# Two stores of one attention and mixture kernel, divided by rows between two DMA queues

## The chip, the cores and the metric

The kernel runs on one core of a Trainium2 chip. A core has a matrix engine (TensorE, PE in the profile), a vector engine (VectorE, DVE), a scalar engine (ScalarE, ACT), a general engine (GpSimd, POOL) and one that does little but issue transfers (SyncE, SP). Sixteen DMA engines move data between the chip's memory and the core's on-chip memory, which has 128 rows, called partitions. Transfers are issued by GpSimd, SyncE or ScalarE, each with a queue of its own on the DMA engines. The metric is the device time of one execution in microseconds (us), less is better.

## The reference

Inputs are `q`, `k` and `v` of 4 x 6400 x 256 float32 numbers and small weights. The first half is attention across channels: with columns of `q` and `k` normed over the 6400 positions, each batch has a 256 x 256 matrix, its softmax, and a product with `v`. The second half sends each of the 25600 rows of that result to two of eight small experts.

```python
qn = q / (np.linalg.norm(q, axis=1, keepdims=True) + 1e-06)
kn = k / (np.linalg.norm(k, axis=1, keepdims=True) + 1e-06)
s = kn.transpose(0, 2, 1) @ qn / tau
...
x = v @ softmax(s)                        # then, by rows of x:
logits = x @ w_gate                       # the two largest of 8, softmax over them: w
out = x + sum over the two of w * ((x @ A[e]) @ B[e])
```

(The last three lines are a summary.) In bytes: three inputs of 26.2 MB are read and an output of 26.2 MB is written.

## The kernel before, in words

A batch's 6400 positions are laid out as 128 partitions of 50 rows, so that partition p holds positions 50p to 50p + 49. Work goes by "chunks", one row of every partition at a time.

For `q` and `k` of a batch there are three loads each (`QK`: 17, 17 and 16 chunks), some cut in two (`PARTS`). GpSimd issues them (`do_load`, L578) and they convert float32 to bfloat16 on the way. TensorE sums `k`-by-`q` products and diagonal norms in two accumulators (`do_G`, L593, L597, L602). Some norms are taken instead by ScalarE squares and VectorE sums (`do_sq` L615, `do_add` L621). At the end of a batch a short chain gives the softmax: `accs` (L651), `rsqrt`, `s` (L710), `exp` (ScalarE, L715), transposition (L729), and products with the weights (`waA`, L755, L757).

For `v` a batch has five loads of 10 chunks, also by GpSimd. A tile of `v` is transposed on TensorE (`do_T`, L788), copied (`do_Te`), multiplied by gate and expert weights (`ZL`, `log`, `Z`), gated on VectorE, and multiplied by the attention matrix (`do_Y`, L915 and L920). `do_Ye` copies the result into a `y` tile of 128 x 10 x 256 float32, by ScalarE (L769) or VectorE (L771). There are seven such tiles.

A `y` tile is stored as one transfer of 128 rows of 10240 bytes (`do_store`, L928), or, for the last two tiles of the last batch, in three parts. SyncE issues all stores, one behind the other. Tile (b, i) is the i-th of batch b.

The order of all this is not written by hand. `make_plan` lists every step with its dependencies, an estimated cost and a due time, `Plan.run` plays it through as a simulation and yields one list of steps, and the program emits them in that order; the order on each engine is then fixed. Some stores are held back on purpose: `HOLD` names a load for a store, and a tiny transfer by SyncE (`do_hold`, L645) waits for that load, so that this store and those behind it wait too. Tile (0, 2) is the first that is stored, at 76.65 us. Tile (0, 0) is held for the load of `k` (3, 1), and issued at 167.45 us.

Hardware queues tell completion by counts: a transfer adds sixteen in all to its semaphore, and the program uses eight such semaphores in turn for the transfers of SyncE and ScalarE. Whoever next writes a `y` tile waits until its store has completed.

Of the kernel before, what the change touches and what calls it, by code (L numbers as in the profile page):

```python
# [32 lines left out]
class Clock:  # L33


    WINDOW, FIRST, LOW, HIGH = 3.413, 0.31, 0.5, 0.8

# [3 lines left out]
    def at(self, t):  # L41
        w = max(0, int((t - self.FIRST) / self.WINDOW) + 1)
        while len(self.cold) <= w:
            share = self.busy[-1] / self.WINDOW
            self.cold.append(share < (self.HIGH if self.cold[-1] else self.LOW))
            self.busy.append(0.0)
        return w

    def took(self, t, us):

        end, w = t, self.at(t)
        while us > 1e-9:
            pace = 2.0 if self.cold[w] else 1.0
            step = min(us * pace, max(self.FIRST + w * self.WINDOW - end, 1e-6))
            self.busy[w] += step
# [5 lines left out]
    def idle(self, t):  # L61

        w = self.at(t)
        return t - self.FIRST - (w - 1) * self.WINDOW - self.busy[w] > self.SPARE

# [165 lines left out]
def make_plan(B, order, ahead):  # L231
# [150 lines left out]
    for b in range(B):  # L382
        for i in range(NP):
            x = pos["v", b, max(g for g, (i0, _) in enumerate(V) if i0 <= i)]
            parts = UNITS if b == B - 1 and i >= NP - FINE else ((0, PC),)
            for c, n in parts:
# [25 lines left out]

PARTS = {(0, 0): ((0, 2), (2, 15)), (0, 2): ((34, 8), (42, 8)), (3, 2): ((34, 8), (42, 8))}
FINE = 2
FIRST = 4
OFF = {(0, 0, 'k'), (0, 0, 'q'), (0, 1, 'q'), (0, 2, 'k'), (0, 2, 'q'), (0, 4, 'q'), (0, 5, 'q'),
        (0, 6, 'k'), (0, 6, 'q'), (0, 7, 'k'), (0, 8, 'q'), (1, 0, 'k'), (1, 0, 'q'), (1, 1, 'q'),
# [41 lines left out]
def kernel(  # L459
# [11 lines left out]
    nc = tc.nc  # L471

    B, N, C = q.shape
    P = 128
# [15 lines left out]
    out_v = out.rearrange("(b p c) d -> b p c d", b=B, p=P)  # L490
# [44 lines left out]
    held = {}  # L535
# [25 lines left out]
    def do_load(s, what, b, i, c, n):  # L561
        if what == "v":
            t, src, c0 = sb(s, "v", (b, i), [P, PC * max(n for _, n in V), C], BF16), v_v, c
        else:
            t = sb(s, "qk", (what, b, i), [P, max(n for _, n in QK), C], BF16)
            src, c0 = {"q": q_v, "k": k_v}[what], QK[i][0]
            if (b, c) == (0, 0):
                n = FIRST
                if "first" not in W:
# [6 lines left out]
        if (what, b, i) in (("q", 0, 0), ("k", 0, 0)):  # L576
            c, n = FIRST, c + n - FIRST
        nc.gpsimd.dma_start(t[:, c - c0:c - c0 + n, :], src[b, :, c:c + n, :])  # L578
# [346 lines left out]

    def do_store(s, b, i, c, n):
        lo = i * PC + c
        nc.sync.dma_start(out_v[b, :, lo:lo + n, :], held["y", (b, i), ""][:, c:c + n, :])  # L928


    do = dict(load=do_load, wts=do_wts, sq=do_sq, add=do_add, red=do_red, n2p=do_n2p, hold=do_hold, warm=do_warm, cast=do_cast, G=do_G, accs=do_accs, n2=do_n2, rsqrt=do_rsqrt, rq_ps=do_rq_ps, s=do_s,
              exp=do_exp, recip=do_recip, aT_ps=do_aT_ps, aT=do_aT, waA_ps=do_waA_ps, waA=do_waA,
              a=do_a, ZL=do_ZL, ZLe=do_ZLe, T=do_T, Te=do_Te, log=do_log, loge=do_loge, Z=do_Z, Ze=do_Ze, gzT=do_gzT,
              gzTe=do_gzTe, Y=do_Y, Ye=do_Ye, store=do_store)
    for name in ("m1", "eq1", "lm", "m2", "mask", "msum", "t", "th", "g2"):
        do[name] = gate_step(name)
# [50 lines left out]
```

## Time and profile before

| what | value |
|---|---|
| time, median of 3 runs | 254.43 us (254.37 to 254.54) |
| span of the profiled run | 252.7 us |
| TensorE busy | 217.8 us, 86% of the span |
| VectorE busy | 192.7 us, 76% |
| ScalarE busy | 151.1 us, 60% |
| GpSimd busy | 27.1 us, 11% |
| stores of 1280 KB by SyncE | 18, median 16.7 us from issue to landing |
| loads of `v` by GpSimd | 20 of 640 KB (as written), median 20.5 us to landing |
| ScalarE's own transfers | 3, all in the first 2 us |

The profile is of one execution. Busy times count an engine's instructions, and not what it spends on issuing transfers or waiting. The profile has the transfers by packet as well: their queue, their size, and when each began and ended. A queue is named q0 for GpSimd's loads, q1 for SyncE's transfers and q10 for ScalarE's; q8 and q14 fetch instructions for the engines themselves.

### The profile page before, as it was taken

What the parts mean: (1) busy time and instruction counts of PE and PEld (TensorE: products, weight loads), DVE (VectorE), ACT (ScalarE), POOL (GpSimd) and SP (SyncE); (2) the same over time, 40 slices, a digit from 0 to 9 for tenths busy, and PEclk for the clock granted to TensorE, in tenths of its full rate; (3) what the DMA queues carried; (4) which work ended last, traced back from release to release, by engine and by line L of the source; (5) the groups of instructions that cost most, each with busy time, mean ns of one, the idle gap of its engine ahead of it and who ended that gap; (6) DMA issues with size and microseconds to landing.
All of it is one profiled execution on the core that took longest, in us unless ns stands there. A gap on an engine that the chain in (4) does not pass through costs nothing.

```text
span 252.7 us, 5852 instructions
## 1 busy us (share of the span) xinstructions
PE 217.8 (86%) x2357; PEld 193.0 (76%) x2357; DVE 192.7 (76%) x528; ACT 151.1 (60%) x269; POOL 27.1 (11%) x54
## 2 busy tenths in 40 slices
PE   0274995988999998689999999889999979999990
PEld 0162882876999996579899899779999769999980
DVE  0055589869899987588899899489898898889850
ACT  5454427546786543975667768362674846657671
POOL 7003010040002002000500100500000000000000
PEclk9998899999999999999999999999999999999997
DMA  8999999999999999999999999999999999999996
GB/s 251 217 217 209 211 223 208 217 218 215 215 217 241 303 305 298 224 213 221 210 215 220 215 217 217 211 212 313 317 251 353 322 341 317 337 392 415 404 408 249
DMA packets 11243, 66.70 MB, mean 264 GB/s; under 512 B 1360, under 2 KB 1744, under 8 KB 6608
## 3 DMA queue, kind: packets, MB, share of 16 engines
q0 software_dynamic: 6912, 38.80, 74.4%
q1 hardware_dynamic: 3968, 26.87, 26.1%
q10 hardware_dynamic: 336, 0.66, 0.8%
q8 instruction: 18, 0.29, 0.4%
q14 instruction: 9, 0.07, 0.1%
HBM read 78.91 MB, written 26.21 MB: 416 GB/s over the span
## 4 chain that ended last, share of the span: by engine, by line
PE 53%; DMA 32%; issue 5%; DVE 4%; ACT 2%; POOL 1%; POOLq 0%; DVEq 0%
DMA v<-in_v_dram 18%; PE Y_ps L915 13%; PE acc L593 10%; DMA qk<-in_q_dram 10%; PE Y_ps L920 6%; PE T_ps L788 5%; PE ZL_ps L812 5%; DMA qk<-in_k_dram 5%; PE gzT_ps L902 4%; PE acc L597 3%; PE acc L602 2%; PE Z_ps L879 1%; ACT a_exp L715 1%; DVE a_bf L763 1%; PE log_ps L826 1%
## 5 line engine op out<-in xcount | busy, mean ns | idle before, releaser
L593 PE MATMUL acc<-qk 128*128 128x256 bf16 x400 | 69.6, 282 | 17.0 <-DMA qk<-in_k_dram 9.4
L915 PE MATMUL Y_ps<-a_bf,vT 128*128 128x256 bf16 x400 | 60.0, 273 | 0.2 <-DVE acc_sb L710 0.2
L621 DVE TENSOR_TENSOR ssq<-ssq,sq 128x1280 f32<-128x1280 f32 (+1 forms) x27 | 43.4, 1606 | 19.6 <-ACT sq L615 19.6
L769 ACT COPY y<-Y_ps 128x512 f32<-128x512 f32 x79 | 46.2, 586 | 16.6 <-PE Y_ps L920 13.5
L593 PEld LDWEIGHTS <-qk 128*128 128x128 bf16 x400 | 34.2, 101 | 20.7 <-DMA qk<-in_k_dram 11.5
L615 ACT ACTIVATE sq<-qk 128x1280 f32<-128x1280 bf16 (+1 forms) x27 | 36.9, 1368 | 17.7 <-DVE ssq L621 16.6
L915 PEld LDWEIGHTS <-vT 128*128 128x128 bf16 x400 | 38.9, 98 | 4.7 <-issue 0.3
L920 PE MATMUL Y_ps<-ball,gzT 128*128 128x256 bf16 x200 | 38.2, 273 | 0.0
L597 PE MATMUL acc<-qk 128*128 128x128 bf16 x242 | 34.5, 224 | 0.0
L788 PE MATMUL T_ps<-ident,v 128*128 128x128 f32 x200 | 27.6, 274 | 0.6 <-DVE waA_sb L757 0.4
L769 ACT COPY vT<-T_ps 128x512 f32<-128x512 f32 (+1 forms) x44 | 21.2, 510 | 10.9 <-PE T_ps L788 10.5
L597 PEld LDWEIGHTS <-qk 128*128 128x128 bf16 x242 | 24.4, 101 | 3.5
L890 DVE TENSOR_TENSOR gz<-zl,gateg 128x256 bf16<-128x256 f32 x70 | 26.3, 445 | 0.3
L578 POOL DMA_DIRECT2D v<-in_v_dram x20 | 11.5, 576 | 133.7 <-PE T_ps L788 92.8
L788 PEld LDWEIGHTS T_ps<-ident,v 128*128 128x128 f32 x200 | 22.3, 141 | 1.6 <-DVE waA_sb L757 0.6
L602 PE MATMUL acc<-qk 128*128 128x128 bf16 x168 | 23.4, 222 | 0.0
L902 PE MATMUL gzT_ps<-ident,gz 128*128 128x128 f32 x100 | 20.9, 281 | 2.6 <-DVE gateg L868 1.4
L920 PEld LDWEIGHTS <-gzT 128*128 128x128 bf16 x200 | 19.6, 98 | 2.3
L812 PE MATMUL ZL_ps<-waA_sb,vT 128*128 128x136 bf16 x280 | 19.5, 223 | 1.7 <-DVE waA_sb L757 1.5
L771 DVE COPY gzT<-gzT_ps 128x256 f32<-128x256 f32 (+1 forms) x40 | 15.0, 380 | 7.1 <-PE gzT_ps L902 5.6
L812 PEld LDWEIGHTS <-vT 128*128 128x128 bf16 x280 | 17.7, 98 | 2.4 <-issue 2.1
L615 ACT ACTIVATE ssq<-qk 128x1536 f32<-128x1536 bf16 x8 | 11.9, 1489 | 11.4 <-DMA qk<-in_q_dram 7.4
(80 smaller groups left out, 271.3 us busy)
## 6 DMA issues: line engine op xcount, KB each, us to landing
out_dram<-y SPq DMA_DIRECT2D x18, 1280.0 KB, 16.7
v<-in_v_dram POOLq DMA_DIRECT2D x20, 640.0 KB, 20.5
qk<-in_q_dram POOLq DMA_DIRECT2D x7, 1088.0 KB, 23.7
qk<-in_k_dram POOLq DMA_DIRECT2D x7, 1088.0 KB, 28.4
qk<-in_q_dram POOLq DMA_DIRECT2D x4, 512.0 KB, 19.2
qk<-in_k_dram POOLq DMA_DIRECT2D x4, 512.0 KB, 22.5
qk<-in_q_dram POOLq DMA_DIRECT2D x2, 1024.0 KB, 19.4
qk<-in_k_dram POOLq DMA_DIRECT2D x2, 1024.0 KB, 23.8
```

The costliest lines, as they stand in the source:

```text
L593: nc.tensor.matmul(acc[ic][:, 0:256], kt[:, j, ic::CC], qt[:, j, :], start=c == 0, stop=False, skip_group_check=True)
L597: nc.tensor.matmul(acc[ic][:, 256:384], kt[:, j, ic::CC], kt[:, j, ic::CC], start=False, stop=False, skip_group_check=True)
L602: nc.tensor.matmul(acc[ic][:, 384:512], qt[:, j, ic * P:(ic + 1) * P], qt[:, j, ic * P:(ic + 1) * P], start=False, stop=c == NC - 1, skip_ ...
L615: nc.scalar.activation(out[:, 0:n, :], t[:, j:j + n, :], ACT.Square)
L621: nc.vector.tensor_tensor(out=t, in0=t, in1=held["sq", (w, b, g), ""][:, 0:n, :], op=OP.add)
L769: nc.scalar.copy(out, in_)
L788: nc.tensor.matmul(ps[:, j, :], vt[:, c + j, :].bitcast(FP32), W["ident32"], is_transpose=True, start=(j == 0), stop=(j == n - 1))
L812: nc.tensor.matmul(ps[:, j, :], vT_of(b, i, c + j)[:, :, ic], st[b]["waA"][:, ic, :], start=(j == 0 and ic == 0), stop=(j == n - 1 and ic ...
L890: nc.vector.tensor_tensor(out=pairs[:, h].rearrange("p c (e r) -> p c e r", e=E), in0=z[:, 2 * h:2 * h + 2, :].rearrange("p c (e r) -> p c ...
L902: nc.tensor.matmul(ps[:, j, :], pairs[:, j * P:(j + 1) * P], W["ident32"], is_transpose=True, start=(j == 0), stop=(j == n // 2 - 1))
L915: nc.tensor.matmul(ps[:, j, :], vT_of(b, i, c + j)[:, :, ic], st[b]["a"][:, ic, :], start=(j == 0 and ic == 0), stop=False, skip_group_che ...
L920: nc.tensor.matmul(ps[:, j, :], pair[:, :, j], W["B"], start=False, stop=(j == 1), skip_group_check=True)
```

## The change

Two tiles are stored in three transfers instead of one. SyncE stores rows 0 to 111, then ScalarE stores rows 112 to 119 and rows 120 to 127. The tiles are (0, 2), the first store of all, and (0, 0). The bytes written, their addresses and their source are the same.

[...]

```diff
 PARTS = {(0, 0): ((0, 2), (2, 15)), (0, 2): ((34, 8), (42, 8)), (3, 2): ((34, 8), (42, 8))}
 FINE = 2
+SPLIT = {(0, 2): (112, 8, 8), (0, 0): (112, 8, 8)}
 FIRST = 4
...
     def do_store(s, b, i, c, n):
         lo = i * PC + c
-        nc.sync.dma_start(out_v[b, :, lo:lo + n, :], held["y", (b, i), ""][:, c:c + n, :])
+        p = 0
+        for rows in SPLIT.get((b, i), (P,)):
+            eng = nc.scalar if p else nc.sync
+            eng.dma_start(out_v[b, p:p + rows, lo:lo + n, :], held["y", (b, i), ""][p:p + rows, c:c + n, :])
+            p += rows
```

The planner knows nothing of `SPLIT`, so its list of steps stays as it is. On TensorE, VectorE and GpSimd the instructions and their order are unchanged. On ScalarE four transfers come in. The first two stand behind a square of `q` (L615, in the profile before at 76.52 us) and ahead of a copy of `zl` (L769, at 77.69); the other two stand behind a copy of `zl` (at 170.31) and ahead of a square (L615, at 172.60). SyncE has as many instructions as before. The next writer of each of the two `y` tiles now waits for three completions. As four more transfers take their turn at the eight semaphores, later transfers use other ones than before, each waiting for the transfer that used it last.

## The prediction, made before the changed kernel ran

> **What bounds the kernel now.** I read the DMA part of the page first, since the change moves nothing but stores.
>
> ```profile
> span 252.7 us, 5852 instructions
> ...
> DMA  8999999999999999999999999999999999999996
> ...
> q0 software_dynamic: 6912, 38.80, 74.4%
> q1 hardware_dynamic: 3968, 26.87, 26.1%
> q10 hardware_dynamic: 336, 0.66, 0.8%
> q8 instruction: 18, 0.29, 0.4%
> q14 instruction: 9, 0.07, 0.1%
> ```
>
> The queue lines are packets, megabytes and share of sixteen engines' span; the shares add to 101.8%. The sixteen DMA engines are busy from the first microsecond to almost the last. The third and fourth lines are loads (q0) and stores (q1); q8 and q14 are refills of instructions, small in bytes. Then the windows (busy time by engine, granted clock, DMA share, GB/s), to see whether this holds in every stage:
>
> ```profile
> 20.00:70.00 50.00, 41.57 (x420) 33.89 (x418) 39.45 (x96) 27.08 (x42) 6.97 (x12) 0.97 1.04 215
> 70.00:110.00 40.00, 36.06 (x402) 32.45 (x400) 33.06 (x87) 24.90 (x45) 4.24 (x8) 1.00 1.03 262
> 110.00:165.00 55.00, 53.66 (x577) 49.08 (x575) 46.40 (x128) 37.02 (x66) 8.48 (x16) 1.00 1.04 216
> ...
> 196.00:220.00 24.00, 21.71 (x251) 19.12 (x250) 20.77 (x77) 16.30 (x39) 1.59 (x3) 1.00 1.03 333
> 220.00:238.00 18.00, 18.00 (x217) 16.95 (x215) 16.24 (x54) 11.59 (x25) 0.00 (x0) 1.00 1.02 403
> 238.00:253.00 15.00, 8.77 (x85) 7.63 (x82) 4.91 (x14) 6.80 (x14) 0.00 (x0) 0.87 0.79 323
> ```
>
> The DMA share stays at 1.02 to 1.04 until 238 us (packets of one engine overlap a little, hence over 1). TensorE is close behind: full from 110 on. So two resources could own the end. The end itself says which: the stores issued from 238 us on with their time to landing, and, from SyncE's waits after 183 us, what it waits for last (us, times, longest).
>
> ```profile
> L928 SPq DMA_DIRECT2D out_dram<-y x7: 332/332/333, 239.0 to 247.4; - x7
> ...
> DMA to landing us min/median/max: 4.5/5.0/6.7
> ```
>
> ```profile
> SPq L982 <- DMA out_dram<-y: 3.8, 5, 1.2
> ```
>
> The last store is issued at 247.42, and its last engine lands at about 252.0, 0.7 before the span ends. A completion is sixteen counts, one an engine, and the trace has the time of each. For this last store six engines count at 249.9 to 250.1, two at 250.3 and 250.4, six at 250.7 to 251.1, and the last two at 251.7 and 252.0. So 2.5 us after the issue is the unhindered landing, and the rest is backlog on ten engines.
>
> Where does unequal backlog come from when every load and store gives each engine eight rows? I chained the packets: in a full queue an engine's next packet starts 19 ns before the end of a load's packet, or 4 ns before the end of a store's, so packets can be joined into sixteen chains. From 22 us up to 238 no chain has a hole over 0.1 us. The 18 packets of q8 (16 KB, 0.89 to 0.99 us each) lie on only eight chains, in turn: two chains have three, six have two. The q14 packets (8 KB, some 0.3 us) lie on the other eight, nearly all on two or three of them. Idle holes near 239 us exist on those other eight alone: five of 0.7 to 1.5 us, one of 0.1, none on two. That is the pattern 2, 6, 2, 6 of the landings: two engines with a third refill, six with two, two with only small refills but several, six with time to spare. An engine that took a third refill ends about 0.95 us later (251.85 against 250.9 on average). So the time is the total work of the two busiest DMA engines.
>
> [...]
>
> **The change, part by part.**
>
> 1. *Rows moved.* Two stores of 128 rows become 112 + 8 + 8. [...] A row is one packet of 10240 B: 385 ns in the last stage (381 from start to start), 398 beside loads (380 net). Over two stores an upper engine loses 2 x 0.38 = 0.76 us, a lower one gains 0.76 and four completion packets of 9 ns: 0.80 us. There is no hole for it to vanish in until 238 us.
> 2. *ScalarE's issues.* Four more DMA issues. Its three in this trace took 0.36 to 0.46 us, so 0.4 each, 0.8 a pair. By the new order the first pair stands behind the square at 76.52 and ahead of the copy of `zl` at 77.69; that copy may move to 78.5 and end at 78.9, but VectorE, its reader, is in its sum until 79.43, and ScalarE itself next idles 1.39 us for that sum. The second pair stands behind the `zl` copy at 170.31, and ScalarE then idles 1.90 us until 172.60, again for VectorE. Cost nothing; at worst one pair in full, 0.8 us of ScalarE time, which would only delay stores that queue for 5 to 36 us anyway.
> 3. *Waits.* The next writers of the two `y` buffers wait for three completions instead of one. For (0, 2) this is near 135 us, 47 us after landing at 87.7. For (0, 0) it is the copy at 180.57; before, the store issued at 167.45 has landed by 178.3. The ScalarE parts are issued about 171; one row behind at most two others' packets on each engine is some 2 us a row at most plus 2.5 for landing, 175 to 178: nothing waits, with 2 us to spare. Behind that copy are four more copies of `y`, and TensorE by its banks; a miss would be about 1 us of TensorE.
> 4. *An earlier load.* ScalarE waits 3.8 us, until 101.52, for a q load; TensorE idles 2.2 us there, for the exponentials that stand behind. If the late engines are relieved by one row, this load lands 0.38 us earlier, and TensorE gains that. It doesn't add to point 1: it brings the last issue forward, and the last store isn't waiting for its issue on the busy engines.
>
> **What decides the sign: which engines are the busy eight.** No view numbers the chains. If they are 8 to 15: the two worst go from 252.0 and 251.7 to 251.24 and 250.94, the six from 251.1 to 250.34; below, the two with q14 packets go from 250.4 to 251.2, and the six early ones, five of them with holes of 0.7 to 1.5 us, absorb most of 0.80 or end at 250.9 at the latest. The maximum is 251.24, and the end comes 0.76 us earlier: 254.43 - 0.76 = 253.67.
>
> I take this case. What speaks for it: refills lie in two sets[...], so a division into halves is likelier than a scatter; and the two groups would then come out level within 0.04 us. That TensorE's eight are the upper ones is my choice, about three to one, and not read from any line.
>
> **Rivals.**
>
> - *The busy eight are the lower half, or interleaved with a worst engine in it.* Nothing speaks against it but the choice above. The worst engine gains 0.80: 252.0 to 252.8, and 254.43 + 0.80 = 255.2. If only the second worst is low: 251.7 + 0.8 = 252.5, 254.9.
> - *The gain is taken by the lower engines or a new wait.* If the k = 8 parts cost more than their rows (0.2 us an engine and store), the q14 engines end at 251.6, the gain is 0.4 and the time 254.0, within 0.2% (0.51 us) of no change. Against it: the 9 ns of a completion packet.
> - *TensorE owns the end.* Then only the 0.38 of point 4 counts, 254.05. Against it: the unhindered landing is at 250.1, 1.9 us before the real one.
> - *Both halves of the gain add,* or refills fall a little otherwise: 253.3 as a lower bound.
>
> **How the numbers follow.** Upper half busy, 0.74: 253.67, told as 253.7, with 253.3 to 253.9 about it. Gain lost or TensorE's, 0.08: 254.0 to 254.4. Lower or interleaved, 0.18: 254.9 to 255.2. For 8 in 10 the range takes the first two, with half a row's slack above: 253.3 to 254.6; the third is left out. Faster by over 0.2% is below 253.92: 0.74; same 0.08; slower 0.18.
>
> **What would show it.** Right: the last store's late counts come 0.7 to 0.8 us earlier and closer together (2.1 us of spread to about 1.2), the number of out_dram issues grows by four ACT rows of 80 KB, SyncE's last wait for out_dram shrinks, and holes near 239 us shrink on the six idle engines. Point 2 is wrong if ScalarE's `zl` copies at 77.7 or 170.3 hold up VectorE; point 3 if the copy near 180.6 names out_dram. The forecast is wrong if the last two counts move to 252.5 or later: then the busy engines are the ones that got the extra rows.

## The result, and the profile after

| | before | after |
|---|---|---|
| median of 4 runs | 254.49 us (254.37 to 254.69) | 256.0 us (255.83 to 256.71) |
| ratio, 95% interval | | 1.0064 (1.0044 to 1.0084) |
| span of the profiled run | 252.7 us | 254.2 us |
| issue of the last store, its last count | 247.42, 252.0 | 248.93, 253.3 |

The change makes the kernel 1.5 us slower, where 0.8 us less was forecast. The page of the kernel after, its queues (packets, megabytes, share of sixteen engines' span) and one group of its transfers (KB each, median us to landing):

```profile
span 254.2 us, 5860 instructions
...
q0 software_dynamic: 6912, 38.80, 74.2%
q1 hardware_dynamic: 3936, 26.54, 25.7%
q10 hardware_dynamic: 400, 0.99, 1.3%
...
out_dram<-y SPq DMA_DIRECT2D x2, 1120.0 KB, 11.8
```

Thirty-two rows have gone from q1 to q10, as the change says: 64 more packets there, half rows and half completions. Their share of sixteen engines' span rose from 0.8% to 1.3%, by some 20 us of engine time, where 32 rows of 0.39 us are 12.5. That is the first sign.

Where the rows went can be read from the packets, joined end to end into sixteen chains. Each of ScalarE's parts has eight row packets, eight completion packets of 4 bytes, and nine counts, the first ahead of its rows (for (0, 2) at 77.4 and 77.8 us, the first row at 80.05); every transfer of SyncE and ScalarE in the kernel before has sixteen counts. Between 76.5 and 100 us thirteen chains show seven rows of the 112 outright, and ScalarE's sixteen rows of (0, 2) lie on eight of the chains, two on each. So eight engines carry nine rows of that tile and the others seven, where each carried eight; that was the aim of the change. The engines that gain rows are the "lower" ones of the prediction, and the low ones below; those that lose rows are its "upper" or "8 to 15", and the high ones below. No trace shows such numbers.

The stores' issues (minimum, median and longest ns, first and last start):

```profile
L932 SPq DMA_DIRECT2D out_dram<-y x24: 332/333/882, 76.7 to 248.9; - x24
L932 ACTq DMA_DIRECT2D out_dram<-y x4: 288/339/579, 76.7 to 171.9; - x4
```

The last one starts 1.5 us later than before, and the last store's sixteen counts lie at 251.5 (six), 251.6 (two), 252.0 to 252.3 (four), 252.6, 253.1, 253.2 and 253.3. Its unhindered landing is 2.6 us after the issue, against 2.5 before. The tail on some engines is still there, 1.8 us instead of 2.0. So both the issue and the backlog moved, and each has to be explained. Windows of the kernel before (busy time, instructions, granted clock, DMA share, GB/s):

```profile
104.00:108.00 4.00, 3.56 (x39) 3.11 (x38) 3.41 (x8) 3.21 (x6) 0.00 (x0) 1.00 1.01 209
170.00:182.00 12.00, 12.00 (x149) 11.23 (x147) 11.27 (x29) 5.45 (x12) 0.00 (x0) 1.00 1.04 319
```

and of the kernel after:

```profile
104.00:108.00 4.00, 3.67 (x21) 2.73 (x22) 2.14 (x6) 3.12 (x7) 0.00 (x0) 0.57 1.00 206
170.00:182.00 12.00, 11.81 (x153) 11.16 (x153) 10.80 (x26) 5.46 (x11) 0.00 (x0) 1.00 1.03 293
```

Two places stand out. From 104 to 108 us TensorE ran at 0.57 of its clock and did 21 matmuls instead of 39: the `q` load that ScalarE waits for landed at 101.9 instead of 101.5, and TensorE's hole ahead of its work grew from 2.25 to 2.64 us. (Whether the longer hole is what cut the clock is not shown: in a run below, "one", it was cut as well, to 0.72, after a hole of 2.15 us.) From 170 to 182 us the DMA engines were as busy as before, but moved 293 GB/s instead of 319: (319 - 293) x 12 us is 0.31 MB, about 1.0 us of all sixteen engines. Busy engines that move less have longer packets. This is ScalarE's queue, by packet, in the trace after; a row of 10240 bytes usually takes 385 or 398 ns:

```
80.0 to 83.6 us:  792 744 1507 1216 1295 773 and ten of 385 or 398
175.2 to 178.0 us: 1129 1309 947 2059 1666 916 1019 and nine of 385 or 398
```

### The profile page after: what moved, and what is told of

Its sections match the earlier page's. It is cut to its first block, busy times and chain, and to the rows that moved or that the text cites. A ratio compares the mean times of both kernels' runs of the same rounds, so it can differ in the third digit from the quotient of the medians.

```text
span 254.2 us, 5860 instructions
## 1 busy us (share of the span) xinstructions
PE 219.3 (86%) x2357; PEld 193.6 (76%) x2357; DVE 192.7 (76%) x528; ACT 151.1 (59%) x269; POOL 27.0 (11%) x54
## 4 chain that ended last, share of the span: by engine, by line
PE 45%; DMA 40%; issue 6%; DVE 3%; ACT 2%; POOL 1%; POOLq 0%; DVEq 0%
DMA v<-in_v_dram 17%; DMA qk<-in_k_dram 13%; PE Y_ps L916 12%; DMA qk<-in_q_dram 10%; PE acc L594 7%; PE Y_ps L921 6%; PE T_ps L789 5%; PE ZL_ps L813 4%; PE gzT_ps L903 4%; PE acc L598 2%; PE acc L603 1%; PE Z_ps L880 1%; POOL qk L579 1%; ACT a_exp L716 1%; PE log_ps L827 1%
## 5 line engine op out<-in xcount | busy, mean ns | idle before, releaser
L916 PE MATMUL Y_ps<-a_bf,vT 128*128 128x256 bf16 x400 | 61.0, 276 | 0.2 <-DVE acc_sb L711 0.2
```

The source lines that it names most:

```text
L916: nc.tensor.matmul(ps[:, j, :], vT_of(b, i, c + j)[:, :, ic], st[b]["a"][:, ic, :], start=(j == 0 and ic == 0), stop=False, skip_group_che ...
```

## The experiments

Three theories came from this. A: the late `q` load and the cut clock make TensorE late, and that comes out at the end. B: the row moved loads the wrong engines. C: the divided stores' own packets are slow. The first four runs divide them. Each group of runs was measured together with the kernel before, whose medians are 254.37 to 254.40 us.

**One division at a time, and one queue.** The edits to the kernel after:

```diff
-SPLIT = {(0, 2): (112, 8, 8), (0, 0): (112, 8, 8)}
+SPLIT = {(0, 2): (112, 8, 8)}                        # first only
+SPLIT = {(0, 0): (112, 8, 8)}                        # second only
+SPLIT = {(0, 2): (112, 16), (0, 0): (112, 16)}       # even load
-            eng = nc.scalar if p else nc.sync
+            eng = nc.sync                            # SyncE alone
```

> Only tile (0, 2) is divided; (0, 0) goes as one transfer. Theory A (the first division makes the q load that ScalarE waits for near 101.5 us land late, TensorE's hole grows to 2.2 to 2.3 us, its clock is cut for some us, and everything after is 1.3 us later): TensorE's matmuls and the load issues after 116 us stand 1.2 to 1.3 us later than before, and the time is 255.5 to 255.8. Theory B (the extra rows alone load three engines that take refills, and the end is those engines' work): about half of the 1.5 us, 255.2 or less, and no shift at 116 us. Theory C (the second division, with its slow 10240-byte packets between 175 and 180 us, costs it): 254.2 to 254.6.

> Only tile (0, 0) is divided. Theory A: nothing happens near 101.5 us, the load issues after 116 us stand where they stood before within 0.1 us, and the time is 254.0 to 254.6. Theory B: about 255.2. Theory C: 255.7 to 256.0, with ScalarE's packets of 1 to 2 us between 175 and 180 us.

> Both tiles are divided in the same three parts, but SyncE issues all of them, in its one queue. [...] Theory A needs only a load that lands some tenths later, so it says the time depends on where that load lands here: if ScalarE's wait near 101.5 us ends at 101.9 or later, 255.6 to 256.0; if it ends at 101.5, 254.3 to 254.8. Theory B (rows): as with ScalarE, 255.7 to 256.1. Theory C' (a third queue on the engines makes the slow packets): no packets of 10240 bytes of 0.7 us or more in the divided stores, 254.0 to 254.6.

> Both tiles go as 112 rows by SyncE and one transfer of 16 rows by ScalarE, which gives each of the sixteen engines one row: no engine carries more than before. Theory B (rows moved to the wrong engines): no change, 254.3 to 254.7. Theory C' (a third queue, with packets of neighbouring rows): 255.2 to 256.0, with ScalarE's packets again slow, some at 0.7 to 2 us. Theory A: as for e3, it goes with the end of ScalarE's wait near 101.5 us.

| run | median (lowest to highest), executions | ratio to before, 95% interval | last issue, last count, span |
|---|---|---|---|
| first only | 255.71 (254.59 to 258.4), 17 | 1.0056 (1.0036 to 1.0075) | 248.78, 251.9, 253.0 |
| second only | 254.88 (254.25 to 257.5), 20 | 1.0026 (1.0011 to 1.0041) | 246.93, 251.5, 252.6 |
| SyncE alone | 254.88 (254.51 to 255.56), 9 | 1.0024 (1.0014 to 1.0035) | 246.84, 251.8, 252.7 |
| even load | 255.61 (254.83 to 256.38), 5 | 1.0045 (1.0025 to 1.0065) | 247.45, 251.9, 253.0 |

No theory's numbers came out whole. The 42 executions of before measured with them lie between 254.22 and 254.99; three of these four kernels spread over 1.5 to 3.8 us. A trace is of one execution, so it must be read with its own time: the one of first only is of an execution of 254.75 us. It settles A all the same. The `v` load that GpSimd issues when TensorE frees a tile (in brackets: idle before, and what ended it) stands thus in the kernel before,

```profile
114.61 0.53 POOL L578 DMA_DIRECT2D v<-in_v_dram  x1 [15.97 <-PE T_ps L788]
```

thus in the kernel after,

```profile
115.87 0.53 POOL L579 DMA_DIRECT2D v<-in_v_dram  x1 [17.17 <-PE T_ps L789]
```

and thus in first only:

```profile
116.00 0.53 POOL L579 DMA_DIRECT2D v<-in_v_dram  x1 [17.39 <-PE T_ps L789]
```

First only has the late load, the cut clock (0.67 from 104 to 108 us) and a TensorE that is even later than in the kernel after, and its last store is issued at 248.78. Yet its last count is at 251.9, no later than before: the backlog on the engines reached that far anyway. A TensorE that is 1.4 us late is hidden behind it, so A is out as the cause of the end. (In the kernel after, too, the unhindered landing at 251.5 is well ahead of the last count at 253.3.) Nor was the landing of the load an effect of the change: in second only, where nothing differs until 165 us, it came at 100.9, against 101.5 in the trace of before.

Even load, which moves no row from one engine to another (its ScalarE parts have sixteen rows and sixteen completion packets each, 32 packets of that queue from 76 to 90 us), costs as much as first only, so B alone is out too. SyncE alone has the same parts on the same partitions as the kernel after, and costs much less.

**A second trace, the partitions, the turn of semaphores, and a candidate.** Three things were then to be told apart. ScalarE's parts read eight neighbouring partitions, 112 to 119 and 120 to 127. That the packets are slow because these lie side by side was a guess; no trace showed it so far. The run "apart" reads partitions 4 apart for the same transfers: if the guess is right, its rows are all at their usual length, which is the first case expected of it below. It leaves out the right rows: rows 112 to 127 of the two tiles come out as copies of others, as they also do in the runs "four" and "one" below.

```diff
+            q0 = {112: slice(3, 32, 4), 120: slice(35, 64, 4)}.get(p, slice(p, p + rows))
-            eng.dma_start(out_v[b, p:p + rows, lo:lo + n, :], held["y", (b, i), ""][p:p + rows, c:c + n, :])
+            eng.dma_start(out_v[b, p:p + rows, lo:lo + n, :], held["y", (b, i), ""][q0, c:c + n, :])
```

The turn run is the kernel before, with one load of weights in three parts, as shown here; the candidate divides (0, 0) alone, by SyncE, and cuts that load into seven:

```diff
-        nc.sync.dma_start(W["A0"], moe_A.rearrange("e (p g) r -> p e g r", g=8))
+        for e in ((0, 4), (4, 6), (6, 8)):
+            nc.sync.dma_start(W["A0"][:, e[0]:e[1]], moe_A.rearrange("e (p g) r -> p e g r", g=8)[:, e[0]:e[1]])
```

> The changed kernel once more, for a second trace of it. Theory P (packets of ScalarE's eight-row transfers, and others, take up to 2 us instead of 0.4, by differing amounts from execution to execution, and the engines' lost time is what comes out at the end): the sum of the time that packets of 4 to 16 KB take above their usual is well above the 9 us of before, and the span above before's 252.7 us goes with it, about one sixteenth of the sum plus 0.2 us. Theory R (only the rows moved and TensorE's shift count): the trace repeats the first one, 254.2 us with the last count 253.2 to 253.4, whatever the sum.

> The same three transfers of both tiles, of the same sizes, to the same places of the output, by the same queues; but ScalarE's two read partitions 3, 7, ... 31 and 35, 39, ... 63 of the tile instead of 112 to 119 and 120 to 127, so that rows 112 to 127 of these two tiles hold copies of other rows. [...] ScalarE's 32 packets of 10240 bytes all take 0.38 to 0.40 us, and the median falls to 254.5 to 255.0. Theory of the third queue, or of the output's side: packets of 0.7 to 2 us as before, and 255.7 to 256.2.

> The kernel before, with no tile divided; one load of weights in the first microseconds goes in three parts instead of one, so that two more transfers take their turn at the eight semaphores. Theory of the turn (the last lines wait for the eight semaphores in a fixed order, 0.06 us each, and the last store now uses the second of the order and not the eighth): the time from the last store's last count to the end of the span grows from 0.7 to 1.1 us, and the median is 254.7 to 254.9, as tight as before. Theory that the turn does not matter: 254.3 to 254.5.

> Only tile (0, 0) is divided, all three parts by SyncE, and the load of weights goes in seven parts, so that with eight more transfers the last store has the eighth semaphore again. By the refills seen in the traces the two worst engines lose a row and end at 251.3 to 251.6, three others gain one and end at 251.5, against 252.0: if these two theories (turn and refills) hold, 253.9 to 254.1. If slow packets set the end, 254.4 to 255.2.

| run | median (lowest to highest), executions | ratio to before, 95% interval |
|---|---|---|
| after, again | 256.66 (255.2 to 258.03), 9 | 1.0084 (1.0058 to 1.0109) |
| apart | 254.73 (254.47 to 255.18), 20 | 1.0015 (1.0008 to 1.0022) |
| turn | 254.82 (254.63 to 255.15), 19 | 1.0015 (1.0008 to 1.0022) |
| candidate | 254.62 (254.14 to 256.28), 12 | 1.0016 (0.9999 to 1.0032) |

*Apart.* Only the partitions that are read differ, and 1.9 us of the median are gone, and the spread with them: the slowest of its 20 executions (255.18) is ahead of the fastest of the kernel after (255.2). The DMA queues from 170 to 182 us in the kernel after (packets, MB, share of sixteen engines):

```profile
q0 software_dynamic: 310, 1.13, 50.6%
q1 hardware_dynamic: 263, 2.20, 45.6%
q10 hardware_dynamic: 32, 0.16, 6.6%
```

and in the run "apart":

```profile
q0 software_dynamic: 336, 1.27, 52.3%
q1 hardware_dynamic: 279, 2.36, 48.3%
q10 hardware_dynamic: 32, 0.16, 3.3%
```

The same 32 packets and bytes of ScalarE's queue take half the time, and no 10240-byte packet of that queue takes over 0.4 us in the whole trace. The loads and stores beside them get more through. So theory C holds: ScalarE's packets were slow where the eight partitions of a transfer lay side by side (13 of 32 rows took 0.74 to 2.06 us), and none of 32 was where they lay four apart. Why neighbouring partitions are slow is not shown. It isn't that they are high partitions: the complete version below reads 96, 100, ... 126, also high, and has no row packet over 0.4 us from 165 to 182 us.

The third queue has a part in the size of the loss. A third queue alone doesn't make packets slow, as the run "apart" has one too. But SyncE alone reads the same neighbouring partitions, has two such packets (1.04 and 0.95 us near 177.7), and is only 0.5 us slower than before. The large loss was seen only where both came together. In the candidate, by SyncE too, two packets took 0.93 and 1.15 us near 177.7. Its median missed the 253.9 to 254.1 that were forecast for it; the neighbouring partitions don't explain that, since the run "one" below, with partitions four apart, is hardly faster (254.54).

*After, again.* Here the slow packets were worst at 80 to 85 us, up to 1.5 us. The next `k` load landed at 108.2, before at 107.0, and the loads after it stayed 0.6 to 2.4 us late up to 200 us; TensorE was not late (the `v` load at 114.22), and the last count came at 252.9. The expectation had the size wrong: what packets of 4 to 16 KB took above their usual sums to 15.0 us against 8.6 before (from 20 us on, packets over by more than 0.05), and a sixteenth of the difference, with the 0.2 of the turn below, gives a span of 253.3, not the 253.8 measured. For the first trace the same sum is 29.4 us, which gives 254.2, as measured; for the run "apart" it is 7.3. The sixteenth part is the average engine's, and the end waits for the slowest one: in the first trace the sixteen counts of the last store are spread over 1.8 us, and SyncE's wait for it ends at 253.28, with the last of them (253.26).

*Turn.* At the end SyncE waits for the eight semaphores in a fixed order. In the trace of before the last store has the eighth (S118), and the drain follows at once:

```
before: 250.09 S116  251.33 S117  251.97 S118  252.03 drain
turn:   252.09 S108  252.15 S109  252.21 S110  252.27 S111  252.33 S112  252.39 S113  252.45 S118  252.52 drain
after:  253.28 S110  253.34 S111  253.40 S116  253.46 S117  253.52 S118  253.59 drain
```

With two transfers more the last store has the second of the order, and six waits follow that are long fulfilled, 0.06 us each: 0.37 us. In the waits of SyncE after 183 us (us, times, longest) before's five became

```profile
SPq L983 <- DMA out_dram<-y: 4.1, 2, 3.5
```

since one long wait now covers landings that had one each. The median went up by 0.4 with no store divided at all. The kernel after has four transfers more, so its last store has the fourth semaphore, and four such waits follow: 0.25 us of its loss.

**The map of the refills, and the gain by itself.** With partitions and turn known, the rows can be tested. No view says which engine a packet was on; the packets have to be joined end to end, and where two end together the joining is a choice. In the chains of the trace after, ScalarE's row packets mark the low eight engines. When each chain is held to its eight rows of every load, the refills of q8 (the prediction calls them TensorE's; whose they are no view shows) fall on two of these and on six of the others, both in the trace after and in that of four tiles; the two engines with a third refill are among the others. This is the map. (The expectations below reckon with three low and five high. Their sums need only one low engine at 251.1.) Four tiles divided is twice the dose; one tile is half of it. Both read partitions four apart for the eight-row parts, go by SyncE, and make eight transfers more, so that the turn is as before. The complete version writes every row of the output rightly: its four parts are rows 0 to 95, sixteen rows in steps of two, and twice eight in steps of four, for which the division seen in the trace after would again give nine rows on each low engine and seven on the others (an estimate, not read from its trace).

```diff
+SPLIT = {(0, i): (112, 8, 8) for i in range(4)}      # four
+SPLIT = {(0, 0): (112, 8, 8)}                        # one, loads of weights in seven parts
+SPLIT = {(0, 0): (slice(0, 96), slice(97, 128, 2), slice(96, 128, 4), slice(98, 128, 4))}   # complete, in six parts
```

> Four tiles, (0, 0) to (0, 3), go as 112 + 8 + 8 rows, all by SyncE, and the two eight-row parts read partitions 3, 7, ... 31 and 35, 39, ... 63[...]; the output's rows 112 to 127 of these tiles hold copies of other rows. Eight more transfers than before, so the last store has the last semaphore, as before. What is left is the rows[...]. Theory of the map read from the traces[...]: those three end at 251.1 + 4 x 0.4 = 252.7, against 252.0 before, so 255.0 to 255.2. Theory of the prediction (the eight engines with refills are the upper eight): the worst end at 252.0 - 1.5 = 250.5 and the end is the idler engines', 250.4 + 1.6 = 252.0 at most: 254.0 to 254.5.

> As the four, but tile (0, 0) alone, with the loads of weights in seven parts so that again eight more transfers are made. Rows 112 to 127 of that tile hold copies of other rows. Theory of the map: the two worst engines lose one row (252.0 to 251.6), the three low ones with refills gain one (251.1 to 251.5), so 253.9 to 254.1, and with no slow packets nearly as tight as before. If a division costs something of its own[...]: 254.4 or more.

> A complete version: tile (0, 0) goes by SyncE as rows 0 to 95, then the sixteen rows 97, 99, ... 127, then the eight rows 96, 100, ... 124 and the eight rows 98, 102, ... 126[...]. The loads of weights go in six parts, eight more transfers in all. [...] 253.9 to 254.2. If the sixteen rows[...] crowd too: 254.3 to 254.8, with packets of 0.6 to 0.8 us among them.

Four: 255.17 us (255.07 to 255.29, ratio 1.003, 1.0018 to 1.0042), with the last count at 252.67; the forecast had said 252.7 for a low engine with refills. The four latest counts are 251.7, 251.9, 252.2 and 252.7, the rest 251.0 or earlier. In the joined chains all four are low engines, those with the extra rows. So with four rows more on each low engine the kernel is slower (255.17 against 254.37), not faster.

One: 254.54 (254.3 to 254.81, ratio 1.0005, 0.9997 to 1.0014), and complete: 254.49 (254.31 to 254.84, 1.0004, 0.9995 to 1.0013). They miss the forecasts (253.9 to 254.1 and to 254.2) by 0.4 and 0.3. The complete one lies where it was put if the sixteen rows are slow too, but none of the slow packets that were to show this is there. The traces point elsewhere: the second load of `k` lands at 14.6 and 14.4 instead of 13.9, and loads up to 78 us stay up to 0.8 us late, mostly about 0.5. So the weights in small pieces, which only were to set the turn, may cost what the row brought. The next run tests this. (In "one" a row packet still took 1.02 us at 175.7, on partitions four apart; what made it slow is not shown.)

**The same without the pieces.** The complete version, with the weights in one load and five transfers of 64 bytes in their place:

```diff
+        for j in range(5):
+            nc.sync.dma_start(first[0:1, 9 * C + 128 + 16 * j:9 * C + 144 + 16 * j], moe_B[0, j:j + 1, 0:16])
```

> As the complete version before it, but the load of weights is whole again, and the five further transfers that bring the last store back to the eighth semaphore carry 64 bytes each. The seven- and six-part loads of weights had put the loads of q and k 0.5 us later from 14 us on. If that, and nothing else, hid the gain of one moved row: loads land as before (the second of k at 13.9 us), and the median is 253.9 to 254.1. If a division costs something of its own: 254.3 to 254.6 again.

The second load of `k` lands at 14.1, and those from 68 to 78 us where they did before. It takes 254.14 us (253.98 to 254.28, 13 executions), ratio 0.9989 (0.9981 to 0.9998): 0.26 us, or 0.1%, below before, and just above the 253.9 to 254.1 expected. No run has the five small transfers without the division, so that the gain is the row's rests on the sum. The first line of its page:

```profile
span 252.4 us, 5868 instructions
```

and SyncE's waits after 183 us:

```profile
SPq L986 <- DMA out_dram<-y: 4.0, 5, 1.2
```

The five waits are back, and the last count is at 251.66 instead of 251.95; the map had said 251.6.

## Why the prediction was wrong

The bound was read rightly: the end is the work of the busiest DMA engines. First only shows it from the other side, with TensorE 1.4 us late and the last count where it was.

The step that cost most is a term of point 1. A row of an eight-row part was taken at its usual 0.38 us; 13 of the 32 packets took longer, up to 2.06 us. Together the 32 took 10.2 us more than usual, on eight engines, before the loads and stores beside them are counted. The rival "If the k = 8 parts cost more than their rows (0.2 us an engine and store)" was there, but small, and "the 9 ns of a completion packet" was no evidence against it: that is the shortest of ScalarE's completion packets before (9 to 29 ns), and it says nothing of rows that eight engines read from neighbouring partitions. (Its "k = 8 parts" are those of eight rows.) Partitions four apart took 1.9 us off the median (256.66 to 254.73).

The other step that failed is "What decides the sign": "That TensorE's eight are the upper ones is my choice, about three to one, and not read from any line." These are the eight engines with q8's refills. By the joined chains some are low, and one low engine that lands at 251.1 is enough. The worst two do go down by 0.76 from 252.0, but this low one goes up by 0.80, to 251.9. With this map the prediction's own sum gives 0.1 us of gain instead of 0.76, so 254.3, still inside its range: this step took the gain away, but not the time out of the range. Interleaved engines were among the rivals, but priced as if a low one were already among the two latest (252.5 to 252.8); what counts is the highest low one after the move. Four tiles divided, with partitions four apart, show it by itself: 252.67 where the sum says 252.7. So the sign of being wrong that was named beforehand, last counts of 252.5 or later, did come (252.6 to 253.3), but not for the reason named with it: the rows alone lead to 251.9.

A third term was missing. The section on the change says that later transfers use other semaphores than before, and the prediction doesn't ask in which order they are waited for at the end. That is 0.25 us by the trace.

Of the 0.33 us that the run "apart" is slower than before, 0.25 is thus the turn, and 0.1 is left for the rows, where the map says -0.1. That difference is within what its executions vary. In the first measurement the whole loss was 1.5 us, in the second 2.3; both lie in the range of its executions.

Point 2 held: ScalarE's two issues at 76.72 and 171.58 start beside its square and copy, and the next copy starts at 77.76 (77.69 before). Point 3 held, with little to spare: it put the landing of ScalarE's parts of (0, 0) at 175 to 178, they landed at 177.6 and 180.0, the SyncE part at 180.1, and the next writer of that tile starts at 181.84, behind TensorE and not behind a store. Its "one row behind at most two others' packets" was an estimate; by the joined chains, of ScalarE's 16 rows of (0, 2), 15 follow a packet of a store, and all 16 stand ahead of a packet of a load. Point 4 did not show: the landing of that load varies by more between traces (100.7 to 102.1 in the first six) than the 0.38 it was to gain.

What stays open: in the trace after, loads of 4096 bytes were slow as well from 169.8 to 172.2 us (up to 0.87 us instead of 0.32), before ScalarE's second pair was on the engines. They make up some 7 of the 21 us by which the first trace's sum is above before's, so about a third of that surplus is not explained by the eight-row parts. It occurs, weaker, in the traces of first only and of "one", the other two with a late TensorE; no run was made to find its cause. It is also open why rows from neighbouring partitions were slow, and whether partitions four apart would help SyncE alone, for two tiles. Nor was it tried how much of the slowness comes from a transfer's own rows and how much from the transfers beside them.

## What to carry to other kernels

Look at which partitions a small transfer reads, not only at how many rows it gives each engine: here, on eight neighbouring partitions and by a queue beside the stores' own, 13 of 32 rows took 0.74 to 2.06 us, and on partitions four apart none took over 0.4. Before balancing engines, find out from the trace which engines are the late ones, with a dose in a kernel of its own if no view numbers them. And see where added transfers leave whatever goes round in turn: two more moved the last store from the eighth semaphore to the second, and six waits of 0.06 us each came behind it.

## What was not expected of the hardware

- A row of 10240 bytes usually took 0.385 or 0.398 us. Where ScalarE's parts read eight neighbouring partitions (the trace after), 13 of 32 rows took longer, up to 2.06 us; with partitions four apart none of 32 took over 0.4.
- The refills of instructions on q8 (18 packets of 16 KB, 0.88 to 1.23 us each in the trace after) go round eight of the sixteen engines, by the joined chains two of the low eight and six of the others.
- At the end of the program each wait for a semaphore that was already there took SyncE 0.06 us (the turn run, 252.09 to 252.45 us).
- From 104 to 108 us TensorE's granted clock was 0.57, 0.67 and 0.72 after holes of 2.64, 2.88 and 2.15 us (the kernel after, first only, "one"); after one of 2.25 us, before, it stayed at 1.00. So in these four traces the length of the hole alone doesn't decide it.
